# Group 0's head in pieces: a half-and-half load of x and of the modulation weights, q, k and v by half groups, and a new order of all engines

## The chip, the core and the metric

The kernel runs on one core of a Trainium2 chip. The core has five engines with instruction queues of their own: TensorE (PE in the profile; its weight loads are shown as PEld), VectorE (DVE), ScalarE (ACT), GpSimd (POOL) and SyncE (SP), which here issues nearly all DMAs. They run side by side and meet at semaphores. The metric is the device time of one execution in microseconds (us). Three runs of the kernel before gave 236.53, 236.69 and 236.71; their median is 236.69.

## The reference

A transformer block on x of 2048 rows by 512 columns, bfloat16, with six modulation vectors made from a condition vector c:

```
mod = (silu(c) @ w_mod).reshape(1, 6, 1, 512)        # sa, ca, ga, sb, cb, gb
h = layernorm(x) * (1 + ca) + sa
q, k, v = split(h @ wqkv)                            # 32 heads of 16
logits[s, w] = q[s] . k[s - 2 w] / 4,  w = 0..7      # masked where s - 2 w < 0
o = softmax over w, times v[s - 2 w]
x = x + ga * (o @ wo)
h = layernorm(x) * (1 + cb) + sb
x = x + gb * ((gelu(h @ w_gate) * (h @ w_up)) @ w_down)   # 1792 wide
```

The attention looks at eight keys only, at distances 0, 2, ... 14. Its products are made elementwise on VectorE; TensorE sums them over the 16 elements of a head with a 0/1 matrix.

## The kernel before

The 2048 rows are worked in four groups of 512 (`NSG`, `SG`). For each group there is a set of generator functions, each of which yields operations for one engine: statistics and normalisation of the first layernorm (`ln1`, `ln1_x`, `norm_act`), its transposition (`transp0` for group 0, `transp` for the others, by TensorE or by a transposing DMA), scale and shift into `hT` (`transp0_ev`, `transp_ev`), the twelve qkv products of 512 columns (`qkv`, names `qp.group.block.j`), their eviction by ScalarE (`qkv_ev`, names `qkv.group.block.j`), the way of v through DRAM into shifted copies V4 (`vload`), the products of q and shifted k (`logits`, names `pq`), their sums (`logits_mm`, `lp`, tile LTp), softmax (`soft`; `z`, `e`, `s1`, `ri`, `p`), the transposition of the probabilities (`ptp.0` on TensorE for group 0, a store and four loads through DRAM for the others, `est` and `ptl`/`pt`), products with v (`pv`), their sums (`pv_mm`, `o`, tile o_ps), eviction (`oT`), the projection (`x1_mm`, `x1p`), the second layernorm (`LN2`), and the gated MLP: `g` and `u` chunks, gelu on ScalarE (`gl`), a copy (`ub`), their product on VectorE (`hh`), and the down products `y`.

The order of all operations is written out by hand in the list `ORDER`: a sequence of generator numbers. `Issuer.run` takes the next operation of the generator so numbered and emits its instructions, and so each engine's queue has the order in which its operations come up there. The numbers behind `Op(...)` (a duration, a latency) are not used when the kernel is built. `take` and `give` count buffers: `SL["mm"]` is four PSUM banks that qkv, g, u and y share, `SL["att"]` two, `SL["lg"]` one pair.

What matters for the head, group 0, before the change:

- Loads: rows 256 to 511 of group 0 (`x0.2`) are issued on ScalarE's queue, ahead of c; rows 0 to 255 (`x0.0`) on SP's, then the modulation blocks 1 and 0 (ca, then sa; `wm1`, `wm0`, 512 KB each, lines 242 to 245 and 277 to 281), then wqkv0, x1, wqkv1, x2, wqkv2.
- TensorE first multiplies zeros, so that its clock is up (`warmup`, line 217, tile `warm_ps`, twenty matmuls `w0` to `w19`; the last ones are spread between the first useful pieces).
- The modulation products of block 1 and block 0 go into one tile `mp01` (line 348) and are moved with one addition (`mod01`, line 355).
- The rows are normalised and transposed in two halves (`th0`, `th1`, line 509), scaled and shifted in eight evictions of 256 columns, three on ScalarE (line 545) and five on VectorE (line 543).
- Of the qkv products, two of q (j = 0 and 1) are made in halves of 256 columns, sixteen matmuls (`qkv_halves`, line 580); the other ten are made of 512 columns after both halves of `hT` (line 598).

In the order of TensorE, w11 to w15 stand ahead of the first modulation product, then come th0, the second product, w16, th1, w17 to w19 and then the sixteen half matmuls.

Of the kernel before, what the change touches and what calls it, by code (L numbers as in the profile page):

```python
# [106 lines left out]
def kernel(  # L107
# [113 lines left out]
    def loads():  # L221
# [51 lines left out]
        def act_q():  # L273
            yield Op("ACT", 0.46, ldx(0, 2, 4, nc.scalar), fire="x0.2", lat=mb(0.25), dma=True)
            yield Op("ACT", 0.45, ldc, fire="c", lat=0.0, dma=True)
        qs = [act_q()]
        def head_q():
            yield Op("SP", 0.47, ldx(0, 0, 2), fire="x0.0", lat=mb(0.25))
            for b in (1, 0):
                yield Op("SP", 0.5, lambda b=b: ldwm01(b), take=[SL["prod"]] if b else [], fire=f"wm{b}", lat=mb(0.5))  # L280
        qs.append(head_q())
# [12 lines left out]
        def wd_q():  # L294
            for b in range(4):
                yield Op("SP", 0.65, ldwd(b), fire=f"Wd{b}", lat=mb(0.5 if b < 3 else 0.25), after=[f"qp.{g}.{blk}.3" for g in range(NSG) for blk in range(3)])
# [29 lines left out]
    def mods():  # L326
# [15 lines left out]
        for b in (1, 0):  # L342
            def f(b=b):
                if b:
                    B["mp01"] = T("mm", [P, 8], F32, "modT_ps")
                for ch in range(4):
                    for kt in range(4):
                        nc.tensor.matmul(B["mp01"][:, 4 * b + ch:4 * b + ch + 1],  # L348
                                         lhsT=B["wm01"][:, b, kt, ch * P:(ch + 1) * P], rhs=scT[:, kt:kt + 1],
                                         start=(kt == 0), stop=(kt == 3))  # L350
            yield Op("PE", 0.43, f, after=[f"wm{b}", "scT", "w15"], take=[SL["mm"]] if b else [],
                     give=[] if b else [SL["prod"]], fire=f"mp{b}")
# [220 lines left out]
    def qkv_halves():  # L573
# [11 lines left out]
        for j in range(2):  # L585
            pl.done[f"qp.0.0.{j}"] = pl.done["qph.1.3"]
# [391 lines left out]
```

## Time and profile before

| what | us |
|---|---|
| median of three runs | 236.69 (236.53 to 236.71) |
| span of the profiled execution | 234.1 |
| PE busy | 230.0 (98%), 1387 matmuls |
| DVE busy | 170.4 (73%), 240 instructions |
| ACT busy | 150.0 (64%), 283 instructions |
| POOL busy | 18.6 (8%), 43 instructions |
| twenty warm-up matmuls, line 217 | 7.3 busy |
| sixteen half matmuls, line 580 | 2.0 busy |
| qkv matmuls of 512 columns, line 598 | 42.1 busy, 184 of them |

The page gives the span of the profiled execution and no other time of it; what lies around the span is the difference to the runs, about 2.6 us. Times inside a profile count from the start of the span. A line of the chain in order of time has its start, its length and what it was. A line of a timeline has start, length, engine, source line, instruction, the tiles written and read with their shapes, and in brackets how long the engine had been idle before it and what ended that wait. Ends of matmuls are modelled: they are pipelined, so the distance of their starts says more than their length.

### The profile page before, as it was taken

Reading aid. Unit: us, or ns where it says so; the run is one execution under the profiler, and the core shown is the slowest. Engines: PE = TensorE matmul, PEld = TensorE weight load, DVE = VectorE, ACT = ScalarE, POOL = GpSimd, SP = SyncE. Lnnn points to the kernel's source line nnn. Section 1 sums busy time; section 2 is a strip of 40 time slices with the busy share of each in tenths; the row PEclk is TensorE's granted clock in tenths of the full one; section 3 lists DMA queues with packets and bytes.
Section 4 is the critical chain, followed back from the end, with each engine's and each line's share of the span. In section 5 each row is a group of like instructions: output and inputs, shape, how many; then the busy total and the mean of one; then the engine's idle time right before and its main releaser. Section 6 shows DMA issues by size and latency. Waiting matters only on the chain.

```text
span 234.1 us, 3675 instructions
## 1 busy us (share of the span) xinstructions
PE 230.0 (98%) x1387; PEld 108.2 (46%) x1387; DVE 170.4 (73%) x240; ACT 150.0 (64%) x283; POOL 18.6 (8%) x43
## 2 busy tenths in 40 slices
PE   7999999999999999999999999999999999999995
PEld 2755455434644444444444444444444444444443
DVE  3999999999997999999799788467747421222222
ACT  4899997976997758936656492546754343666400
POOL 2612461000100000100000010000001000000000
PEclk9999999999999999999999999999999999999999
DMA  6997989999969839553102963510000411000011
GB/s 218 373 364 213 202 213 171 276 391 303 176 152 236 291 92 200 98 114 103 56 0 57 202 109 60 156 56 0 0 4 0 90 45 45 3 0 0 0 48 45
DMA packets 36265, 30.21 MB, mean 129 GB/s; under 512 B 14872, under 2 KB 34328, under 8 KB 36248
## 3 DMA queue, kind: packets, MB, share of 16 engines
q1 hardware_dynamic: 35968, 29.72, 50.6%
q10 hardware_dynamic: 280, 0.26, 0.3%
q8 instruction: 11, 0.18, 0.3%
q14 instruction: 6, 0.05, 0.1%
HBM read 22.37 MB, written 4.98 MB: 117 GB/s over the span
## 4 chain that ended last, share of the span: by engine, by line
PE 98%; DVE 0%; issue 0%
PE g_ps L844 21%; PE u_ps L844 21%; PE y_ps L856 19%; PE qkv_ps L598 17%; PE x_ps L811 6%; PE o_ps L790 3%; PE LTp L678 3%; PE warm_ps L217 3%; PE y_ps L868 1%; PE qkv_ps L580 1%; PE hTp L484 1%; PE hTp L509 0%; PE modT_ps L305 0%; PE modT_ps L348 0%; PE gR_ps L369 0%; PE PTp L736 0%
## 5 line engine op out<-in xcount | busy, mean ns | idle before, releaser
L844 PE MATMUL g_ps<-h,Wg 128*128 128x512 bf16 x224 | 57.5, 379 | 0.0
L844 PE MATMUL u_ps<-h,Wu 128*128 128x512 bf16 x224 | 57.5, 379 | 0.0
L878 ACT ACTIVATE gl<-g_ps 128x512 bf16<-128x512 f32 x56 | 33.6, 600 | 24.8 <-PE g_ps L844 23.9
L856 PE MATMUL y_ps<-Wd,hht 128*128 128x512 bf16 x210 | 46.0, 379 | 0.0
L885 ACT CAST ub<-u_ps 128x512 bf16<-128x512 f32 x56 | 32.8, 586 | 18.3 <-PE u_ps L844 18.1
L598 PE MATMUL qkv_ps<-hT,wqkv 128*128 128x512 bf16 x184 | 42.1, 380 | 0.0
L896 DVE TENSOR_TENSOR hht<-gl,ub 128x512 bf16<-128x512 bf16 x56 | 23.0, 421 | 25.3 <-ACT ub L885 25.0
L664 DVE TENSOR_TENSOR pq<-qT,kT 128x4096 bf16<-128x4096 bf16 x16 | 36.3, 2292 | 0.0
L771 DVE TENSOR_TENSOR pv<-PT,V 128x4096 bf16<-128x4096 bf16 x16 | 36.0, 2286 | 0.0
L844 PEld LDWEIGHTS <-Wg 128*128 128x128 bf16 x224 | 21.5, 98 | 27.3 <-issue 2.1
L844 PEld LDWEIGHTS <-Wu 128*128 128x128 bf16 x224 | 21.8, 98 | 26.6 <-issue 0.4
L856 PEld LDWEIGHTS <-hht 128*128 128x128 bf16 x210 | 20.5, 98 | 24.8
L598 PEld LDWEIGHTS <-wqkv 128*128 128x128 bf16 x184 | 20.1, 114 | 19.7 <-issue 3.0
L903 DVE TENSOR_TENSOR ot<-y_ps,x 128x512 bf16<-128x512 f32 x15 | 10.3, 689 | 20.2 <-PE y_ps L856 17.2
L471 POOL TENSOR_TENSOR rstd<-rstd,neghalf 128x4 f32<-128x4 f32 (+1 forms) x9 | 8.8, 980 | 154.1 <-DVE rstd L460 85.5
L527 ACT ACTIVATE h<-h,modT,scl 128x512 bf16<-128x512 bf16 x12 | 8.8, 802 | 11.6 <-DMA h<-xn 11.6
L811 PE MATMUL x_ps<-woP,oT 128*128 128x512 bf16 x64 | 15.3, 379 | 0.0
L430 DVE BATCH_NORM_STATS2 st<-x 128x6 f32<-128x512 bf16 x19 | 12.9, 680 | 3.1 <-DMA x<-in_A_x_dram 2.9
L820 DVE TENSOR_TENSOR x<-x_ps,x 128x512 bf16<-128x512 f32 x16 | 10.8, 686 | 5.0 <-PE x_ps L811 5.0
L801 ACT CAST oT<-o_ps 128x512 bf16<-128x512 f32 x16 | 8.9, 592 | 2.7 <-PE o_ps L790 2.7
L618 ACT CAST qT<-qkv_ps 128x512 bf16<-128x512 f32 x16 | 9.2, 587 | 2.2 <-PE qkv_ps L598 2.1
L620 ACT CAST kT<-qkv_ps 128x512 bf16<-128x512 f32 x16 | 9.5, 596 | 1.2 <-PE qkv_ps L598 1.2
(85 smaller groups left out, 181.5 us busy)
## 6 DMA issues: line engine op xcount, KB each, us to landing
V<-vscr SPq DMA_DIRECT2D x12, 520.0 KB, 10.4
wm<-in_w_mod_dram SPq DMA_DIRECT2D x6, 512.0 KB, 5.4
vscr<-vT SPq DMA_DIRECT2D x4, 512.0 KB, 4.2
out_dram<-ot SPq DMA_DIRECT2D x15, 128.0 KB, 1.7
Wg<-in_B_w_gate_dram SPq DMA_DIRECT2D x1, 1792.0 KB, 11.0
Wu<-in_B_w_up_dram SPq DMA_DIRECT2D x1, 1792.0 KB
wqkv<-in_A_wqkv_dram SPq DMA_DIRECT2D x3, 512.0 KB, 8.3
x<-in_A_x_dram SPq DMA_DIRECT2D x3, 512.0 KB, 8.6
```

The lines of the kernel that those rows point to most:

```text
L430: nc.vector.bn_stats(out=st[:], in_=src()[:, c4, :])
L598: nc.tensor.matmul(ps[:], lhsT=wqkv[blk][:, dt, j::4], rhs=B["hT", sg][:, :, dt, :], start=(dt == 0), stop=(dt == DT - 1))
L664: nc.vector.tensor_tensor(out=pq[:], in0=_ap(B["qT", sg][:, j, :], [[0, W], [1, SG]]), in1=_ap(kT[:, j, sg % 3 * SG + 2:sg % 3 * SG + 2 + ...
L771: nc.vector.tensor_tensor(out=t[:], in0=_ap(B["PT", sg][:, 0, :], [[SG, 2], [0, 4], [1, SG]]), in1=_ap(v[:, 0, j, :], [[8, 2], [4 * (SG + ...
L811: nc.tensor.matmul(ps[:], lhsT=B["oT", sg][:, j, c4::CPS] if sg else B["oT", sg][:, j, c4 * P:(c4 + 1) * P], rhs=woP[:, j, :], start=(j == ...
L820: nc.vector.tensor_tensor(out=x[:, c4, :], in0=B["x1ps", sg, c4][:], in1=x[:, c4, :], op=ALU.add)
L844: nc.tensor.matmul(ps[:], lhsT=Wt[:, dt, ft * P:(ft + 1) * P], rhs=B["h2T", sg][:, :, dt, :], start=(dt == 0), stop=(dt == DT - 1))
L856: nc.tensor.matmul(ps[:], lhsT=B["hh", sg, ft][:, c4 * P:(c4 + 1) * P], rhs=B["Wd", ft // 4][:, ft % 4, :], start=(ft == 0), stop=(ft == F ...
L878: nc.scalar.activation(out=gl[:], in_=B["g", sg, ft][:], func=ACT.Gelu_apprx_tanh)
L885: nc.scalar.copy(out=ub[:], in_=B["u", sg, ft][:])
L896: nc.vector.tensor_tensor(out=hh[:], in0=B["gl", sg, ft][:], in1=B["ub", sg, ft][:], op=ALU.mult)
L903: nc.vector.tensor_tensor(out=ot[:], in0=B["y", sg, c4][:], in1=B["x", sg][:, c4, :], op=ALU.add)
```

## The change

- Both halves of group 0's x are issued on SP, rows 0 to 255 first; ScalarE's queue issues only c.
- Blocks 0 and 1 of the modulation weights are loaded together, in two pieces by rows of w_mod (the inner dimension): `wma` holds rows 0 to 255, `wmb` rows 256 to 511, 1024 columns each. Each piece is multiplied into its own PSUM tile (`mpa`, `mpb`), and the two are added one after the other on VectorE (`mod01a`, then `mod01`).
- The second half's transposes of group 0 use `att` banks like the first half's, no longer `mm` banks.
- All twelve qkv products of group 0 are made in halves of 256 columns, `qu.half.block.u`, where u is a pair of j, each pair in one bank, evicted by one copy of 512 elements (`que.half.block.u`). The first of them, `qh.0` to `qh.3`, go through the four dt of half 0 one by one.
- Fifteen warm-up matmuls instead of twenty.
- `ORDER` is another list: the order of all engines and of SP's queue is new. Of the head TensorE now has: w0 to w5, scp (the transposed silu of c), w6 to w13, mpa, mpb, th0, qh.0, qh.1, th1, qh.2, qh.3, qu.0.0.0, qu.0.0.1, w14, qu.1.0.0, qu.0.1.0, qu.1.0.1, qu.1.1.0, qu.0.2.0, qu.0.2.1, qu.1.2.0, qu.1.2.1, the transposes of group 1, qu.1.1.1, qu.0.1.1, lp.0.0. VectorE has x0, va2 (the variance of ScalarE's part), x1, mod01a, x2, mod01, x3 and then the five writes of hT; behind them three statistics of group 1, three of group 2, the x rows of group 1 and only then pq.0.0. SP has x3 ahead of wm2 and wm3, and the store and reload of ga (`gst2`, `ga`) no longer beside group 0's V4 but between group 3's transposing DMA and Wg. Later, LN2.0's transposes stand after all but two qkv chunks of group 3 (before: all but three), and pv.1.0 to pv.1.2 stand ahead of hh.0.4 on VectorE.

```
-        def ldwm01(b):
-            if "wm01" not in B:
-                B["wm01"] = T("prod", [P, 2, 4, D], BF16, "wm01")
-            nc.sync.dma_start(out=B["wm01"][:, b, :, :], in_=w_mod[:, b * D:(b + 1) * D].rearrange("(t p) n -> p t n", p=P))
+        def ldwm01(a):
+            if a == 0:
+                B["wm01"] = T("prod", [P, 4, 2 * D], BF16, "wm01")
+            nc.sync.dma_start(out=B["wm01"][:, 2 * a:2 * a + 2, :],
+                              in_=w_mod[2 * a * P:(2 * a + 2) * P, 0:2 * D].rearrange("(t p) n -> p t n", p=P))
...
+        qs = [one("ACT", 0.45, ldc, fire="c", lat=0.0, dma=True)]
+        qs.append(one("SP", 0.47, ldx(0, 0, 2), fire="x0.0", lat=mb(0.25)))
+        qs.append(one("SP", 0.47, ldx(0, 2, 4), fire="x0.2", lat=mb(0.25)))
...
+        for a in range(2):
+            def f(a=a):
+                B["mp01", a] = T("mm", [P, 8], F32, "modT_ps")
+                for ch in range(8):
+                    for kt in (2 * a, 2 * a + 1):
+                        nc.tensor.matmul(B["mp01", a][:, ch:ch + 1], lhsT=B["wm01"][:, kt, ch * P:(ch + 1) * P],
+                                         rhs=scT[:, kt:kt + 1], start=(kt == 2 * a), stop=(kt == 2 * a + 1))
...
+                nc.vector.tensor_tensor(out=mod01[:], in0=B["mp01", a][:], in1=mod01[:] if a else c01[:], op=ALU.add)
...
-                        ps = T("mm", [P, len(dts), 256], BF16, "hTp") if half else T("att", [P, 2, SG], BF16, "hTp")
+                        ps = T("att", [P, 4, 256], BF16, "hTp")
...
+    def qkv0(half, blk):
+        ev = [f"LN1.0.h{dt}.{half}" for dt in HB[half]]
+        def mm(u, jj, dt, first, last):
+            nc.tensor.matmul(B["qu", half, blk, u][:, jj, :], lhsT=wqkv[blk][:, dt, 2 * u + jj::4],
+                             rhs=B["hT", 0][:, 2 * half:2 * half + 2, dt, :], start=first, stop=last)
...
+        if half == 0 and blk == 0:
+            for n, dt in enumerate(HB[0]):
+                def f(n=n, dt=dt):
+                    for u in range(2):
+                        if n == 0:
+                            B["qu", half, blk, u] = T("mm", [P, 2, 256], F32, "qkv_ps")
+                        mm(u, 0, dt, n == 0, n == DT - 1)
...
+        for u in range(2):
+            def f(u=u):
...
+                for jj in range(1 if half == 0 and blk == 0 else 0, 2):
+                    for n, dt in enumerate(HB[half]):
+                        mm(u, jj, dt, n == 0, n == DT - 1)
...
+    def qkv0_ev(half, blk):
...
+                nc.scalar.copy(out=o, in_=ps[:])
...
-    pl.spawn(warmup(13, 20))
+    pl.spawn(warmup(13, 15))
```

More of the change, by code (lines that the diff above doesn't have):

```diff
@@ L340, in mods, with f @@
                  act="exp", fire="pre")
[L342 to L352, printed above, removed]
-        def f():
-            nc.vector.tensor_tensor(out=mod01[:], in0=B["mp01"][:], in1=c01[:], op=ALU.add)
-        yield Op("DVE", 0.1, f, after=["mp0", "ident"], give=[SL["mm"]], fire="mod01")
+        for a in range(2):
+            def f(a=a):
[4 more added lines that the diff above has]
+                                         rhs=scT[:, kt:kt + 1], start=(kt == 2 * a), stop=(kt == 2 * a + 1))
+            yield Op("PE", 0.43, f, after=[f"wm{'ab'[a]}", "scT"], take=[SL["mm"]], give=[SL["prod"]] if a else [],
+                     fire=f"mp{'ab'[a]}")
+            def f(a=a):
+                nc.vector.tensor_tensor(out=mod01[:], in0=B["mp01", a][:], in1=mod01[:] if a else c01[:], op=ALU.add)
+            yield Op("DVE", 0.1, f, after=[f"mp{'ab'[a]}", "ident"], give=[SL["mm"]], fire="mod01" if a else "mod01a")
     def mods_g(k):
@@ L546, in transp0_ev @@
                 yield Op("DVE" if onv else "ACT", 0.32 if onv else 0.455, f, after=[f"{ev}.th{half}"] + dep,
-                         take=[SL["hT"]] if dt == 0 and half == 0 else [], give=[SL["mm" if half else "att"]] if n == len(dts) - 1 else [],
+                         take=[SL["hT"]] if dt == 0 and half == 0 else [], give=[SL["att"]] if n == len(dts) - 1 else [],
                          fire=f"{ev}.h{dt}.{half}")
@@ L570 @@
     QKV = [(0, 0), (1, 0), (2, 0), (2, 1), (2, 2), (2, 3), (0, 1), (1, 1), (0, 2), (1, 2), (0, 3), (1, 3)]
-    QKV0 = [(0, 0), (0, 1), (0, 2), (1, 0), (1, 1), (0, 3), (1, 2), (2, 0), (2, 1), (2, 2), (2, 3), (1, 3)]
-    def qkv_halves():
-        for half in range(2):
-            for n, dt in enumerate(((2, 0, 3, 1), (0, 1, 2, 3))[half]):
-                def f(half=half, n=n, dt=dt):
-                    for j in range(2):
-                        if half == 0 and n == 0:
-                            B["qkvps", 0, 0, j] = T("mm", [P, SG], F32, "qkv_ps")
-                        nc.tensor.matmul(B["qkvps", 0, 0, j][:, half * 256:half * 256 + 256],
-                                         lhsT=wqkv[0][:, dt, j::4], rhs=B["hT", 0][:, 2 * half:2 * half + 2, dt, :],
-                                         start=(n == 0), stop=(n == DT - 1))
-                yield Op("PE", 0.218, f, after=[f"LN1.0.h{dt}.{half}", "wqkv0"],
-                         take=[SL["mm"]] * 2 + [SL["q"]] if half == 0 and n == 0 else [], fire=f"qph.{half}.{dt}")
-        for j in range(2):
-            pl.done[f"qp.0.0.{j}"] = pl.done["qph.1.3"]
@@ new lines, in qkv0_done, with f @@
+    def qkv0_done():
+        yield Op("PE", 0.0, lambda: None, after=[f"qu.{half}.{blk}.1" for half in range(2) for blk in range(3)], give=[SL["hT"]], fire="qu")
+    def qkv0_ev(half, blk):
+        for u in range(2):
+            def f(u=u):
+                ps = B["qu", half, blk, u]
+                c0 = half * 256
+                if blk == 1:
+                    o = kT[:, 2 * u:2 * u + 2, 16 + c0:16 + c0 + 256]
+                else:
+                    nm = ("qT", "kT", "vT")[blk]
+                    if (nm, 0) not in B:
+                        B[nm, 0] = T(("q", "", "vs")[blk], [P, 4, SG], BF16, nm)
+                    o = B[nm, 0][:, 2 * u:2 * u + 2, c0:c0 + 256]
+                nc.scalar.copy(out=o, in_=ps[:])
+            yield Op("ACT", 0.485, f, after=[f"qu.{half}.{blk}.{u}"], give=[SL["mm"]], fire=f"que.{half}.{blk}.{u}")
@@ L594, in f, with kq @@
+    def kq(sg, blk, j):
+        return [f"qkv.{sg}.{blk}.{j}"] if sg else [f"que.{half}.{blk}.{j // 2}" for half in range(2)]
+    def qkv(sg):
+        for n, (blk, j) in enumerate(QKV):
             def f(blk=blk, j=j):
@@ L601, in qkv @@
             tk = {0: [SL["q"]], 1: [], 2: [SL["vs"]]}[blk] if j == 0 else []
-            yield Op("PE", 0.856, f, after=[f"LN1.{sg}.h{d}" for d in (("0.1", "1.0", "3.1") if sg == 0 else (2, 3))] + [f"wqkv{blk}"], take=[SL["mm"]] + tk,
+            yield Op("PE", 0.856, f, after=[f"LN1.{sg}.h{d}" for d in (2, 3)] + [f"wqkv{blk}"], take=[SL["mm"]] + tk,
                      give=[SL["hT"]] if last else [], fire=f"qp.{sg}.{blk}.{j}")
@@ L626, in qkv_ev @@
                      fire=f"qkv.{sg}.{blk}.{j}")
-        pl.done[f"qkv.{sg}.l"] = pl.done[f"qkv.{sg}.1.3"]
     def halo():
@@ L635, in f @@
             nc.sync.dma_start(out=vscr[:, :, VH + sg * SG:VH + (sg + 1) * SG], in_=B["vT", sg][:])
-        yield Op("SP", 0.65, f, after=[f"qkv.{sg}.2.3"], give=[SL["vs"]], fire=f"vst.{sg}", lat=1.1)
+        yield Op("SP", 0.65, f, after=kq(sg, 2, 3) + kq(sg, 2, 1), give=[SL["vs"]], fire=f"vst.{sg}", lat=1.1)
         for w4 in range(4):
```

46 lines of the change are left out of this document (25 added, 21 removed), and 70 rows, old and new, of the table ORDER.

## The prediction

> **What bounds it now.** I read the page's summary of the chain that ended last, then that chain in order of time, then timelines of VectorE and ScalarE at the places where the chain could be handed over.
>
> ```profile
> span 234.1 us, 3675 instructions
> PE 98%; DVE 0%; issue 0%
> ```
>
> TensorE is 98% of the chain and waits for nobody: a faster kernel must give TensorE less to do, or let its useful work start sooner. The chain in order of time (start, us, what):
>
> ```profile
> 8.98 0.45 PE hTp L509 x8
> 9.43 0.65 PE warm_ps L217 x3
> 10.07 1.85 PE qkv_ps L580 x16
> 11.93 7.77 PE qkv_ps L598 x36
> ...
> 40.04 0.55 PE PTp L736 x16
> 40.59 0.43 PE LTp L678 x8
> ...
> 62.16 0.89 PE hTp L484 x16
> ...
> 80.66 0.97 PE g_ps L844 x4
> 81.63 0.86 PE u_ps L844 x4
> ```
>
> Two things are to be seen. Until 10.07 useful pieces are mixed with `warm_ps` filler. And the work on 32 columns (LTp, o_ps, PTp) costs more at each change of kind: eight matmuls take 0.55 when they follow full-width work and 0.43 when they follow their own kind, and the four matmuls behind them 0.97 where four otherwise take 0.86. A separate run of such work thus costs 0.12 + 0.11 = 0.23 us.
>
> TensorE is not alone. In the stretch from the first statistics of group 1 to the first transposes of LN2, and in the next:
>
> ```profile
> 10.58:62.16 51.58, 51.58 (x380) 26.03 (x378) 50.95 (x66) 44.99 (x100) 10.34 (x8) 1.00 1.02 265
> 62.16:84.50 22.34, 22.34 (x149) 10.42 (x145) 20.84 (x17) 17.68 (x32) 0.00 (x0) 1.00 0.73 196
> ```
>
> (length; busy PE, PEld, DVE, ACT, POOL; clock 1.00; DMA share; GB/s). VectorE is busy 50.95 of 51.58 us. Whatever starts VectorE late here arrives late at every place where TensorE needs it.
>
> **The change, part by part.** (a) *First qkv matmul.* Now:
>
> ```profile
> 4.12 0.69 DVE L430 BATCH_NORM_STATS2 st<-x 128x6 f32<-128x512 bf16 x1 [2.94 <-DMA x<-in_A_x_dram]
> 8.78 0.17 DVE L355 TENSOR_TENSOR mod<-modT_ps,c 128x8 f32<-128x8 f32 x1
> 8.98 1.68 DVE L543 TENSOR_SCALAR hT<-hTp,mod 128x256 bf16<-128x256 bf16 x5
> 10.58 0.69 DVE L430 BATCH_NORM_STATS2 st<-x 128x6 f32<-128x512 bf16 x1
> 9.91 2.02 PE L580 MATMUL qkv_ps<-hT,wqkv 128*128 128x256 bf16 x16
> 2.36 0.51 SPq L223 DMA_DIRECT2D wqkv<-in_A_wqkv_dram  x1
> wqkv<-in_A_wqkv_dram SPq DMA_DIRECT2D x1, 512.0 KB, 6.6
> ```
>
> The two 256 KB halves of x shared the engines until 4.12. With the first half alone in front I put its landing at 3.65 (between 3.4 and no gain, 4.12). VectorE then has the same chain to the first hT write, which took 8.98 - 4.12 = 4.86, plus one more 0.17 add (mod01 is now summed in two steps); the first x row moved ahead of the variance fix-up delays the second rstd by about 0.3, but the last mod matmuls no longer stand behind transposes. I take the first hT write at 8.65, done 0.40 later, so the first qkv matmul at 9.1 instead of 9.91: **-0.81**. It cannot be before wqkv0 lands, 2.36 + 6.6 = 8.96 (-0.95); with no earlier x it is 9.55 (-0.36). The x half that moves from ACT's queue to SP's puts wm and wqkv0 one issue (0.51) later on SP; that is hidden, since wqkv0 lay 6.6 us in a full queue.
>
> (b) *Second-half transposes* now stand behind the first qkv matmuls instead of ahead: +0.45 after that point. (c) One filler, w14, stays there: 0.65/3 = +0.22; the other fillers go, ahead of that point or with it. (d) *256-column matmuls*: 96 instead of 16 of 256 and 40 of 512 columns.
>
> ```profile
> 10.13 1.80 PE L580 MATMUL qkv_ps<-hT,wqkv 128*128 128x256 bf16 x15
> 11.76 7.93 PE L598 MATMUL qkv_ps<-hT,wqkv 128*128 128x512 bf16 x36
> ```
>
> From 10.13 to 11.76 is 15 spacings of 0.109; one of 512 columns is 7.77/36 = 0.216. Each pair of halves costs 0.002 more, 40 pairs +0.06 (bounds: 0; and 0.6 by 1.85/16, which contains the hand-over from a filler). The twelve evictions keep their form and size, so ScalarE's sum stays.
>
> (e) *New order.* I listed the runs of 32-column work in both orders: 15 before, 12 after, all three saved ahead of LN2 (mp2 joins ptp.0; o.0.0 to o.0.3 sit in two runs): 3 x 0.23 = **-0.69** (0 if the saved hand-overs reappear elsewhere).
>
> With TensorE alone: -0.81 + 0.45 + 0.22 + 0.06 - 0.69 = **-0.77**.
>
> (f) *What is given back.* The second half's hT writes on VectorE begin only after its transposes, themselves behind two pairs of qkv matmuls: 9.1 + 0.44 + 0.45 + 0.2 = 10.2, three of them at 1.68/5 = 0.34, so group 1's statistics start at 11.2 against 10.58, 0.6 late. The new order fills one wait (the x rows of group 1 go ahead of the first pq), and 51.58 - 50.95 = 0.63 of slack is there; I let 0.3 of the 0.6 survive (bounds 0 and 0.6).
>
> ```profile
> 38.29 1.22 DVE L722 TENSOR_TENSOR e<-LTp,rinv 128x1024 bf16<-128x1024 f32 x1
> 61.35 0.73 DVE L448 TENSOR_SCALAR xn<-x,mv,rstd 128x512 bf16<-128x512 bf16 x2
> 62.71 2.78 ACT L527 ACTIVATE h<-hTp,modT,scl 128x512 bf16<-128x512 bf16 x4
> 65.83 0.62 ACT L618 CAST qT<-qkv_ps 128x512 bf16<-128x512 f32 x1
> 66.31 0.63 ACT L620 CAST kT<-qkv_ps 128x512 bf16<-128x512 f32 x1
> 66.95 1.28 ACT L878 ACT_TABLE_LOAD   x1
> 68.25 0.60 ACT L878 ACTIVATE gl<-g_ps 128x512 bf16<-128x512 f32 x1
> ```
>
> First place, ptp.0: e ends at 38.29 + 1.22 + 0.3 = 39.81; TensorE, with one of three runs saved, is there at 40.04 - (0.77 - 0.46) = 39.73: **+0.15** with the semaphore. Second, LN2.0: one qkv chunk more (0.86) now stands ahead of its transposes, so TensorE is there at 62.16 + 0.86 - 0.62 = 62.40; VectorE's xn end at 62.08 + 0.3 = 62.38, no wait. But then only two chunks instead of three cover ScalarE, whose chain runs from the transposes to the first gelu: 68.85 - 62.16 = 6.69, less one eviction (66.31 - 65.83 = 0.48), plus 0.1 for a mod4 copy now in front: 6.3. TensorE needs 0.89 + 6 x 0.86 = 6.05 for the work up to the third gate chunk, which needs the bank that gelu frees: **+0.25**. Later rendezvous (o.1.3, o.2.3) I count at nothing, covered by the VectorE idle shown below; without that cover each is worth 0.2 to 0.35.
>
> The other moves: SP issues x3 before wm2 and wm3 (wm2's product moves from behind group 1's transposes to just ahead of ptp.0, so covered); POOL makes its masks after the two rstd (first use is lp.0.0, behind group 0's 7.77 us of qkv from 11.93 on); the tail of the last group keeps its order. Sum: -0.77 + 0.40 = **-0.37**. The trace's execution gives only its span, 234.1; the runs' median, 236.69, stands 2.6 above it, which I leave as it is: **236.3**.
>
> **Rivals.** *VectorE eats it.* If the whole 0.6 survives, ptp.0 waits 0.45, LN2.0 another 0.15 with 0.25 behind it, and one later o group 0.2: -0.77 + 1.05 = +0.3, 237.0. For it: the 50.95 of 51.58. Against: the reordered x rows.
>
> *Nothing is given back.* qkv at 8.96 and no waits: -0.92, 235.8. For it: TensorE waits nowhere in the present order.
>
> *Slower: group 1's attention weights land late.* The store and reload of ga now sit on SP between group 3's transposing DMA and Wg, and SP waits for the store:
>
> ```profile
> SPq L323 <- DMA gscr<-gR: 3.8, 1, 3.8
> 42.30 1.13 SPq L223 DMA_DIRECT2D Wg<-in_B_w_gate_dram  x1
> 67.67 2.53 SPq L758 DMA_DIRECT2D PT<-escr  x4
> PT<-escr SPq DMA_DIRECT2D x4, 64.0 KB, 3.4
> 74.99 0.43 DVE L896 TENSOR_TENSOR hht<-gl,ub 128x512 bf16<-128x512 bf16 x1 [1.30 <-ACT ub L885]
> 75.33 4.49 DVE L771 TENSOR_TENSOR pv<-PT,V 128x4096 bf16<-128x4096 bf16 x2
> ```
>
> (idle of SP's queue; its issues; the loads' median to landing; VectorE.) Everything up to PT runs through this queue, and a wait of up to 3.8 delays Wg by as much. PT's last load is issued by 67.67 + 2.53 = 70.2 and lands 3.4 later, 73.6 at most; the first pv of group 1 now stands ahead of hh.0.4, in the idle 1.30, that is at 74.99 - 1.30 = 73.7 instead of 75.3. So nothing is spare there, and any lateness of PT delays two pv of 4.49, which end at 78.2. TensorE comes to o.1.1 at about 62.16 + 0.89 + 17 x 0.86 - 0.37 + 0.55 + 2 x 0.43 = 78.7, with 0.5 to spare. If half of the 3.8 reaches PT: 1.9 - 0.5 = 1.4 of wait, -0.37 + 1.4 = +1.0, 237.7; it decides from 0.9 of lateness on. Against: the queue has 67.67 - 42.30 = 25 us to catch up.
>
> *Slower: the clock drops.* Gone fillers leave TensorE idle for about 0.5 before the last mod matmuls and 1.0 before the first qkv.
>
> ```profile
> 1.25 4.88 PE L217 MATMUL warm_ps<-gB 128*128 128x512 bf16 x11 [1.25 <-DVE gB L212]
> 6.17 1.25 PE L217 MATMUL warm_ps<-gB 128*128 128x512 bf16 x5
> ```
>
> The first eleven take 4.88/11 = 0.44 each, later ones 0.216: half speed until about 6.1. A second such stretch of 4.9 us costs 2.4: 238.7. The Trainium skill, "TensorE: Matmul & The Clock Gate", Part 1, says the clock is halved again only after an idle window of about 3.4 us; by that rule the idle here is too short and the time stays as summed. The same page's section on a second failure mode says frequent micro-idles between groups can do it as well; by that the 238.7 would come. No run here shows either yet.
>
> **Numbers.** Chances: forecast (-0.1 to -0.75) 0.46; nothing given back (below -0.75) 0.16; VectorE eats it (-0.1 to +0.5) 0.17; PT late 0.15; clock 0.06. About 0.2%, 0.47 us, is what a measurement of this kernel can tell from no change. Half of the forecast's chance and all of the second lie beyond it: faster 0.23 + 0.16 = 0.39; same 0.23 + 0.15 = 0.38; slower 0.23, with a last 0.02 of the VectorE case. The range goes from a little below the no-wait case, 235.7, to 237.3, which leaves out the clock, half of the PT case and a thin lower edge. The likeliest case's own range is 235.9 to 236.6.
>
> **What would show it.** The first 256-column matmul at 9.1 (wrong if later than 9.6); 12 runs of 32-column work; group 1's statistics on VectorE at 11.2; a TensorE wait of 0.1 to 0.3 ahead of PTp and of about 0.25 in the first gate chunks; the granted clock at 1.00 between 6 and 13 us; pv of group 1 starting before 74 without a DMA as its releaser. The prediction is wrong if TensorE shows waits of over 0.8 in sum behind 12 us, or if group 0's qkv waits for wqkv1 or wqkv2, for which I left nothing.

## The result, and the profile after

The changed kernel is slower: 239.82 us (median) against 236.83 for the kernel before on the same chip, a ratio of 1.011 with a 95% interval of 1.0091 to 1.0128. The ratio leaves out the three slowest of the twenty executions (240.57 to 241.16), which are in the median. Forecast were 236.3 and a range up to 237.3. The profiled execution took 240.34, its span 238.6. The page's summary of the chain of the changed kernel:

```profile
span 238.6 us, 3726 instructions
PE 92%; DMA 3%; ACT 2%; SPq 1%; issue 1%; DVE 0%; ACTq 0%
```

TensorE's share fell from 98% to 92%, and waits for loads came in. TensorE's head in the changed kernel (start, length, what, and in brackets the idle time before and what ended it):

```profile
8.02 0.55 PE L347 MATMUL modT_ps<-scT,wm 128*128 128x1 bf16 x16 [1.04 <-DMA wm<-in_w_mod_dram]
9.39 0.57 PE L347 MATMUL modT_ps<-scT,wm 128*128 128x1 bf16 x16 [0.82 <-DMA wm<-in_w_mod_dram]
9.82 1.01 PE L507 MATMUL hTp<-ident,xn 128*128 128x128 bf16 x8
11.33 1.01 PE L577 MATMUL qkv_ps<-hT,wqkv 128*128 128x256 bf16 x4 [0.50 <-DVE hT L541]
```

Two things are to be seen. Both sets of modulation matmuls wait for their load, and the first 256-column matmul starts at 11.33, not at 9.91 as before or at 9.1 as forecast. And the eight transposes take 1.01 where they took 0.70 and 0.61: the clock is down. The stretches between the changes of the granted clock (the share of full speed at which TensorE was let run; then a stretch's length; busy PE and matmuls; clock; DMA share; GB/s):

```profile
6.18:9.60 3.42, 1.56 (x28) 1.00 1.03 378
9.60:13.01 3.41, 2.91 (x35) 0.50 1.06 378
13.01:16.42 3.41, 3.19 (x17) 0.50 1.09 325
16.42:19.84 3.42, 3.42 (x33) 1.00 1.07 255
```

The clock holds for one stretch of 3.41 us in which TensorE was busy for 1.56, and is then 0.50 for two. VectorE and ScalarE at the places where before they were at 10.58, 38.29 and 62.71:

```profile
14.20 0.69 DVE L428 BATCH_NORM_STATS2 st<-x 128x6 f32<-128x512 bf16 x1
42.56 1.21 DVE L750 TENSOR_TENSOR e<-LTp,rinv 128x1024 bf16<-128x1024 f32 x1
67.38 2.79 ACT L525 ACTIVATE h<-hTp,modT,scl 128x512 bf16<-128x512 bf16 x4
```

They are 3.6 to 4.7 us late, and the span ends 4.5 later: 3.6 is there at 14 us, the half clock until 16.42 adds to it, and what lies behind carries it on. (The times differ by less than the spans. The trace of before is one of that kernel's quicker executions, and the trace of after lies 0.5 above its median. What lies around the span is 1.73 to 1.86 us in every execution of the changed kernel and its variants and 2.15 to 2.33 in the others; but here the span ends 1.3 behind the last landing of a DMA and there 1.0, so this is mostly a matter of where the span ends.) So nearly all of the loss arises before 17 us, and the question is why the loads are late. x itself came as forecast, its first half at 3.52. By the trace's landing events (each of a load's 16 DMA engines reports its end, and the last one counts) the modulation's blocks were there at 5.91 and 7.42 in the kernel before; now its halves are at 7.97 and 9.34. The core's DMA engines from 3.5 to 5.5 us, all engines' busy times first, DMA share and GB/s last; the kernel before:

```profile
3.50:5.50 2.00, 2.00 (x7) 0.61 (x5) 1.34 (x3) 0.90 (x3) 0.00 (x0) 1.00 1.08 364
```

The changed kernel:

```profile
3.50:5.50 2.00, 2.00 (x7) 0.68 (x6) 1.85 (x6) 1.26 (x5) 0.00 (x0) 1.00 0.77 205
```

Right behind x the engines moved 205 GB/s instead of 364. And in the kernel before a load's last engine ends about 0.45 us after its first, in the changed kernel 2.3 us after it (wma: first 5.68, last 7.97).

### The profile page after: what moved, and what is told of

Read it like the earlier page. It is cut to its first block, busy times and chain, and to the rows that moved or that the text cites. A ratio compares the mean times of both kernels' runs of the same rounds, so it can differ in the third digit from the quotient of the medians.

```text
span 238.6 us, 3726 instructions
## 1 busy us (share of the span) xinstructions
PE 230.9 (97%) x1409; PEld 113.6 (48%) x1422; DVE 170.2 (71%) x241; ACT 150.2 (63%) x283; POOL 21.8 (9%) x43
## 4 chain that ended last, share of the span: by engine, by line
PE 92%; DMA 3%; ACT 2%; SPq 1%; issue 1%; DVE 0%; ACTq 0%
PE u_ps L872 20%; PE g_ps L872 20%; PE y_ps L884 19%; PE qkv_ps L627 12%; PE x_ps L839 6%; PE qkv_ps L577 5%; PE LTp L706 3%; PE o_ps L818 3%; DMA wm<-in_w_mod_dram 3%; PE y_ps L896 1%; ACT h L525 1%; PE hTp L507 1%; ACT kT L649 0%; ACT LTp L734 0%; SPq L231 0%
## 5 line engine op out<-in xcount | busy, mean ns | idle before, releaser
L924 DVE TENSOR_TENSOR hht<-gl,ub 128x512 bf16<-128x512 bf16 x56 | 22.4, 421 | 25.9 <-ACT ub L913 25.9
L627 PE MATMUL qkv_ps<-hT,wqkv 128*128 128x512 bf16 x144 | 32.3, 380 | 0.0
L469 POOL TENSOR_TENSOR rstd<-rstd,neghalf 128x4 f32<-128x4 f32 (+1 forms) x9 | 11.7, 1304 | 151.1 <-DVE rstd L458 81.2
L627 PEld LDWEIGHTS <-wqkv 128*128 128x128 bf16 x144 | 15.9, 114 | 15.0 <-issue 1.1
L577 PE MATMUL qkv_ps<-hT,wqkv 128*128 128x256 bf16 x96 | 13.1, 299 | 0.7 <-DVE hT L541 0.5
L577 PEld LDWEIGHTS <-wqkv 128*128 128x128 bf16 x96 | 11.0, 119 | 1.9 <-issue 0.6
```

Source lines behind the costliest of these rows:

```text
L469: nc.gpsimd.tensor_tensor(out=k["rstd"][:, a:b], in0=k["rstd"][:, a:b], in1=neghalf[:, a:b], op=ALU.pow)
L577: nc.tensor.matmul(B["qu", half, blk, u][:, jj, :], lhsT=wqkv[blk][:, dt, 2 * u + jj::4], rhs=B["hT", 0][:, 2 * half:2 * half + 2, dt, :], ...
L627: nc.tensor.matmul(ps[:], lhsT=wqkv[blk][:, dt, j::4], rhs=B["hT", sg][:, :, dt, :], start=(dt == 0), stop=(dt == DT - 1))
L924: nc.vector.tensor_tensor(out=hh[:], in0=B["gl", sg, ft][:], in1=B["ub", sg, ft][:], op=ALU.mult)
```

## The experiments

Medians in us; each ratio, with its 95% interval, is to the kernel before, measured beside it (236.67 to 236.83). The orders of TensorE are given by name; "f" is a filler matmul.

**The clock, or the form of the modulation's pieces?** The first theories: the halved clock costs the time (A); the modulation's halves in rows of 2 KB land late and everything follows from that (B); the order behind the head is worse by itself (C). Fillers that keep TensorE busy in the head:

```
-    w13, mpa, mpb, th0, qh.0
+    w13, 4 f, mpa, 4 f, mpb, th0, 2 f, qh.0
```

> The changed kernel with ten more idle-filling matmuls in the head of TensorE's order: four ahead of the first modulation matmuls, four between the two sets, two between the first transposes and the first 256-column matmul. The loads stay as they are. Theory A (the clock: two windows of 3.41 us at half speed because TensorE was busy for only 1.54 of the 3.40 us before them): the granted clock stays at 1.00 from 6 us on, the eight transposes fall from 0.89 to about 0.45, the work from 10.9 to 16.4 runs at full speed and ends about 2.8 us earlier, group 1's statistics start at 11.3 to 11.8 where they started at 14.20; time 236.8 to 237.4, about the kernel before. Theory B (only the late modulation matters, the clock's share is a by-product that something else gives back): 239.0 to 240.0. Theory C (the order behind the head costs it): group 1's statistics early, but 238.5 or more all the same.

Measured: 238.51 (1.0079, 1.0048 to 1.0109). The clock was 1.00 throughout, and 1.3 us came back, about half of what theory A promised. The time is also the one that theory C names (238.5 or more); but C has group 1's statistics early, and they came at 13.31, not at 11.3 to 11.8, so C stays open here. The loads stayed late (modulation at 8.3 and 9.7), and wqkv's last third with them, which TensorE now met:

```profile
PE qkv_ps L577 <- DMA wqkv<-in_A_wqkv_dram: 1.1, 1, 1.1
```

The modulation by blocks of 1 KB rows again:

```
-                in_=w_mod[2 * a * P:(2 * a + 2) * P, 0:2 * D]
+                in_=w_mod[:, b * D:(b + 1) * D]
```

> The changed kernel with the modulation loaded as in the kernel before, one block of 1 KB rows after the other (block 1, then block 0), the matmuls and additions cut to match; no filler is added. Theory B (the halves by rows in 2 KB pieces land late, at about 8.0 and 9.35): the pieces land at about 6 and 7.5, the first 256-column matmul starts at 9.0 to 9.3 where it started at 11.33. If the clock then holds, the time falls by 2 us for the start and 2.8 for the clock, to 235.0 to 236.5. If the order leaves too little work on TensorE even so (theory A alone), the clock still falls at about 9.6 and the time is 237.5 to 238.5. If the place in the queue and not the form of the pieces makes them late, they land at 8.0 and 9.35 again and the time stays at 239.8.

Measured: 239.60 (1.0111, 1.0080 to 1.0142), landings at 8.32 and 9.72. Theory B falls: the halves by rows are as late as the blocks. Blocks and three fillers ahead of qh.0:

> Block loads as in the second kernel and three fillers between the first transposes and the first 256-column matmul. Theories A and B together: the clock is 1.00 from 6 us on, the first 256-column matmul starts by 9.3, group 1's statistics at about 11.2, and the time is 235.0 to 236.5, below the kernel before by what the prediction's ledger gives (about 0.4, up to 1). Theory C (the new order costs by itself): 237 or more with the clock at 1.00.

Measured: 239.89 (1.0129, 1.0091 to 1.0166), landings at 8.6 and 10.1, clock 0.986. The fillers stood behind the late loads and could not help. The kernel before without its last nine fillers:

```
-        pl.spawn(warmup(13, 20))
+        pl.spawn(warmup(13, 11))
```

> The kernel before without its last nine fillers (those behind the silu transposes and around the modulation's matmuls); loads and everything else as they were. TensorE's real work then fills about 2.1 of the 3.41 us from 6.13 on. Theory A: the granted clock falls to 0.5 at about 9.5 for one or two windows and the time grows by 1.5 to 3 us, to 238.3 to 240; if 2.1 us of work are enough to hold the clock, it stays at 1.00 and the time within 0.3 of 236.8, and the bound lies between 1.5 and 2.1. Theory B: no change, 236.8.

Measured: 237.42 (1.0023, 1.0010 to 1.0036): one window at half clock in the profile and a mean clock of 0.991 to 0.993 in all ten executions, but 0.6 us and not 1.5 to 3. The removed fillers had stood in TensorE's way themselves: the first 256-column matmul started at 9.62, earlier than the 9.91 of the kernel before, and only behind it the half clock cost time (the first one of 512 columns at 12.54 instead of 11.76). The window before the drop in this run:

```profile
5.20:8.61 3.41, 2.14 (x42) 1.00 1.04 356
```

**The queue.** Theory D: the head's loads are late because x and the modulation now go through SP's one queue. What e2 still had different from the kernel before in its loads was the queue of rows 256 to 511, and c going first. Only that load put back on ScalarE's queue, behind c:

```
-        qs.append(one("SP", 0.47, ldx(0, 2, 4), ...
+        qs.append(one("ACT", 0.46, ldx(0, 2, 4, nc.scalar), ...
```

> The changed kernel with one load put back: rows 256 to 511 of x go out on ScalarE's queue again (behind c), not on SP's. Theory D (what is late is not due to the form of the modulation's pieces but to the head's loads now all going through SP's one queue: the modulation's transfers end 2.3 to 2.8 us after their first DMA engine has ended, against 0.45 before): the modulation's halves land at about 6 and 7.5, wqkv's first third at about 9, the first 256-column matmul starts at 9.0 to 9.5, and the time is 235.0 to 237.0 if the clock holds, 237.5 to 238.5 if it still halves at about 9.5. Theory B in what is left of it (halves in 2 KB rows are slow by themselves): they land at 8 or later, and the time stays at 239 to 240.

Measured: 238.35 (1.0078, 1.0053 to 1.0103); landings at 5.86, 7.76 and 9.26 (wqkv's first third), as theory D has it. The time is not as D has it: in the profiled execution the clock held, and it took 238.06 where 235.0 to 237.0 were expected; the first 256-column matmul started at 10.64. The same with blocks:

> The same load put back on ScalarE's queue, and the modulation loaded by blocks of 1 KB rows: all loads of the head then have the form, order and queues of the kernel before, but for c going ahead. Theory D: as the run with rows 256 to 511 alone put back, within 0.5 us. If both the queue and the pieces matter: faster than that run by 1 to 2 us. If neither does (the spread of the landings comes from c ahead of the rest, or from the chip): the modulation lands at 8 or later again and 239 to 240.

Measured: 238.59 (1.0083, 1.0055 to 1.0111); 6.00, 7.44, 8.94: no difference. And e5 with three fillers ahead of qh.0:

> Rows 256 to 511 back on ScalarE's queue, and three filler matmuls between the first transposes and the first 256-column matmul. Theories A and D together: clock 1.00 from 6 us on, first 256-column matmul by 9.5, wqkv's last third landed by 15 us so that TensorE does not wait for it, 235.0 to 236.5: the sum of the prediction. Should the order behind the head cost time of its own (theory C), 237 or more with the clock at 1.00 and the loads on time.

Measured: 237.88 (1.0063, 1.0038 to 1.0088). In its profile the clock held and the modulation was on time (5.74 and 7.44), and it still took 237.63. TensorE started its first 256-column matmul at 10.20, because rows 256 to 511, now behind c and beside the modulation, landed at 6.1 (before: 4.4). The other way round, in the kernel before:

```
-            yield Op("ACT", 0.46, ldx(0, 2, 4, nc.scalar), ...
+            yield Op("SP", 0.47, ldx(0, 2, 4), ...
```

> The kernel before with the one load moved the other way: rows 256 to 511 of x from ScalarE's queue to SP's, behind rows 0 to 255, nothing else. Theory D: the modulation's blocks, at 5.9 and 7.4 in the kernel before, land 2 to 2.5 us later with their engines' ends spread over 2 us or more, the first 256-column matmul starts at 11 to 12 where it started at 9.91, and the time grows by 1.5 to 4 us. If the queue does not matter: 236.8 within 0.3, landings as before.

Measured: 238.00 (1.0059, 1.0039 to 1.0078). This one edit moved the modulation from 5.91 and 7.42 to 7.99 and 9.39, the first 256-column matmul from 9.91 to 11.15, and cut the DMA engines' work at the same place as the change did:

```profile
3.50:5.50 2.00, 2.00 (x9) 0.69 (x8) 1.75 (x6) 1.07 (x4) 0.00 (x0) 1.00 0.63 183
```

So the queue of that one load is the cause of the late loads, shown in both directions. All 18 profiles of this case agree: with x and the modulation on SP's queue alone (five) the modulation's first load landed at 7.97 to 8.62, with one of these loads on ScalarE's queue (thirteen) at 5.70 to 6.14. The time grew by 1.2, less than theory D's 1.5 to 4; the clock, behind the fillers that the kernel before has, held in all four executions.

**What the rest is.** The kernel before without the three fillers right ahead of its first 256-column matmul:

> The kernel before without the three fillers (0.65 us) that stand between the second transposes and the first 256-column matmul; no other edit. It tests term (a) by itself: that a start of group 0's q earlier by x gives x. The transposes end at 9.43, h of block 2 is out by about 9.31 and wqkv's first third landed at 8.95, so the first 256-column matmul starts at 9.43 to 9.5 where it started at 9.91, and the time falls by 0.3 to 0.5 us, to 236.3 to 236.5 (ratio about 0.998). The fillers' place is taken by real work, so theory A sees no drop of the clock. If the start is worth nothing (VectorE's chain of group 1 sets the time behind it): 236.8.

Measured: 236.81 (1.0005, 0.9994 to 1.0016). It says little on term (a): in its profile the modulation's second block landed at 7.87 and wqkv's first third at 9.36, so the matmul started at 9.96. Landings between 7.4 and 8.3 occur in profiles whose head loads are the same; the trace that the forecast was summed on had the earliest. The changed kernel with x's rows 256 to 511 first on ScalarE's queue, then c, and three fillers ahead of qh.0:

> The changed kernel with all head loads on the queues of the kernel before (rows 256 to 511 first on ScalarE's queue, then c; rows 0 to 255 and the modulation on SP's), the halves by rows kept, three fillers ahead of the first 256-column matmul, and the silu transpose two fillers later in TensorE's order since c comes later. Against the run with rows 256 to 511 behind c (237.9) it takes away that load's late landing (6.1 there, 4.4 here expected). Theory D with term (a): modulation at about 6 and 7.5, first 256-column matmul at 9.1 to 9.4 (there 10.20), group 1's statistics at 11.2 to 11.5, waits ahead of the logits' products and of PTp below 0.3 in sum; 236.2 to 236.9. If VectorE's order of the new program is what binds from 12 to 42 us (theory C), the waits on VectorE stay at 0.6 or more and the time is 237.2 to 237.9 however early the start.

Measured: 236.97 (1.0004, 0.9994 to 1.0015), although its profile met a late block (8.01) and a window at half clock. The DMA engines are full again:

```profile
3.50:5.50 2.00, 2.00 (x8) 0.57 (x6) 1.46 (x3) 1.06 (x5) 0.00 (x0) 1.00 1.08 370
```

So the queues and the fillers together bring back 2.85 of the 3.0 us. A 32-column run merged, on top of e9 (the second product with Msum beside the third):

> As the run without the three fillers, and with one more edit: the second of group 0's four products with Msum (8 matmuls of 32 columns by themselves at 46.93) moves behind the next four q, k matmuls, beside the third (48.46). One run of 32-column work fewer, priced in the prediction at 0.23 us: 0.2 to 0.25 us below the run without the three fillers, 236.0 to 236.3, a version faster than both kernels. If VectorE waits for the buffer that this product frees 1.5 us later, the gain goes and 236.4 to 236.9 is left.

Measured: 236.74 (1.0000, 0.9991 to 1.0009). The gain went into a new wait on VectorE, as its second case has it:

```profile
PE o_ps L789 <- DVE pv L770: 0.3, 1, 0.3
```

**Where the forecast gain went.** Another load than x's on the second queue (wma on ScalarE's, both halves of x on SP's):

```
-            nc.sync.dma_start(out=B["wm01"][:, 2 * a:2 * a + 2, :],
+            (nc.sync if a else nc.scalar).dma_start(out=B["wm01"][:, 2 * a:2 * a + 2, :],
```

> The changed kernel with another load than x's on the second queue: the first half of the modulation goes out on ScalarE's queue behind c, both halves of x stay on SP's queue, three fillers stand ahead of the first 256-column matmul. If it is one queue for all loads of the head that spreads the landings (theory D in its general form), rows 256 to 511 land at about 4.2, the modulation at about 6 and 7.5 to 8, wqkv's first third by 9.5, the clock stays at 1.00, and the time is 236.3 to 237.2. If only x's load on the second queue helps (something in that transfer, or the place of the modulation behind both halves of x), the modulation lands at 8 or later and the time is 238 to 239.

Measured: 237.29 (1.0023, 1.0013 to 1.0034), modulation at 6.14 and 7.50. So a second queue keeps the modulation on time, whichever of the two loads uses it; but rows 256 to 511 landed at 5.89, later than expected. Terms (b) and (c) taken back, on top of e10:

```
-    th0, 3 f, qh.0, qh.1, th1, ... qu.0.0.1, f, qu.1.0.0
+    th0, 2 f, th1, qh.0, qh.1, ... qu.0.0.1, qu.1.0.0
```

> The run with all head loads on the queues of the kernel before (236.97), with two of the prediction's terms taken back: (b) the second transposes stand ahead of the first 256-column matmul again, in the place of one filler, and (c) the filler among the 256-column matmuls is dropped. By the ledger -0.38 to -0.45 for (b) if the third rows' normalization is out by 8.7, and -0.22 for (c): 236.3 to 236.5, about 0.2% below the kernel before. If VectorE's waits (0.33 and 0.15 ahead of the logits' products and of PTp) grow by what TensorE comes earlier, nothing is gained: 236.9 to 237.1.

Measured: 237.06 (1.0020, 1.0011 to 1.0028): no gain. Not VectorE, as expected for that case, but three others took it: the loads of modulation block 3 (L304) and of the second half (L346), and, in the middle line, the `att` banks of PSUM, which th1 now shares with th0 and gets only when ScalarE has emptied them:

```profile
PE modT_ps L304 <- DMA wm<-in_w_mod_dram: 0.5, 1, 0.5
PE hTp L506 <- ACT hT L542: 0.5, 1, 0.5
PE modT_ps L346 <- DMA wm<-in_w_mod_dram: 0.3, 1, 0.3
```

What holds VectorE in these runs (theory E) is found in its neighbour. GpSimd's reciprocal root of group 2 in e7:

```profile
18.59 3.32 POOL L468 TENSOR_TENSOR rstd<-rstd,neghalf 128x4 f32<-128x4 f32 x1 [2.38 <-DVE rstd L462]
```

and VectorE in the same run:

```profile
18.75 2.29 DVE L691 TENSOR_TENSOR pq<-qT,kT 128x4096 bf16<-128x4096 bf16 x1
21.94 1.06 DVE L445 TENSOR_SCALAR xn<-x,mv,rstd 128x512 bf16<-128x512 bf16 x3 [0.91 <-POOL rstd L468]
```

In the kernel before the same instruction (first for group 1, then for group 2), not beside a pq:

```profile
13.49 1.02 POOL L471 TENSOR_TENSOR rstd<-rstd,neghalf 128x4 f32<-128x4 f32 x1 [3.12 <-DVE rstd L465]
18.30 1.25 POOL L471 TENSOR_TENSOR rstd<-rstd,neghalf 128x4 f32<-128x4 f32 x1 [3.79 <-DVE rstd L465]
```

It lasts until 0.87 after that pq has ended (18.75 + 2.29 = 21.04; 18.59 + 3.32 = 21.91), and VectorE, itself on the chain from 12 to 42 us there, waits 0.91 for it. The eight profiles of versions with a clock at 1.00 or halved for one window, and with this place of the root, all show it (3.31 to 3.32). The changed kernel as given does not, although a pq starts as soon behind the root there:

```profile
21.80 1.11 POOL L469 TENSOR_TENSOR rstd<-rstd,neghalf 128x4 f32<-128x4 f32 x1 [3.34 <-DVE rstd L463]
21.96 2.29 DVE L692 TENSOR_TENSOR pq<-qT,kT 128x4096 bf16<-128x4096 bf16 x1
```

It is the same in e2 and e3, which like it had the clock halved for two windows. What decides between 1.11 and 3.32 is not shown. Two runs on top of e10, one that moves this instruction and drops the late filler, one that only drops the filler:

```
-    VectorE: x.1.0, x.1.1, x.1.2, vd.2, va.2, x.1.3, pq.0.0
+    VectorE: x.1.0, x.1.1, vd.2, va.2, x.1.2, x.1.3, pq.0.0
```

> The run with all head loads on the queues of the kernel before (236.97), with two edits: the late filler among the 256-column matmuls is dropped, and group 2's reciprocal root (the two statistics instructions on VectorE and the 128x4 one on GpSimd) goes two instructions earlier, between the second and third normalized row of group 1, so that it stands less beside VectorE's first pq (2.29 us). Theory E: with its loads on time the changed order is bound from 12 to 42 us by VectorE, and there by that GpSimd instruction, which takes 3.32 us beside pq where it takes 1.02 and 1.25 in the kernel before, leaving VectorE idle for 0.91. Then VectorE's idle time falls to 0.3 to 0.6, its chain and TensorE's waits ahead of the logits' products and PTp shrink by as much, and the time is 0.3 to 0.5 below the run without these edits: 236.4 to 236.7. If that chain does not bind: 236.7 to 237.0, with only the filler or nothing gained.

> The same run with the first of these edits alone: the late filler (0.22) dropped. If TensorE binds, 236.75; by theory E VectorE binds behind it, TensorE only waits 0.2 longer ahead of the logits' products, and the time stays at 236.9 to 237.0.

Measured: 236.38 (0.9985, 0.9969 to 1.0001) and 237.04 (1.0010, 1.0001 to 1.0018). In e14 the instruction took 1.11, VectorE's wait of 0.91 and TensorE's two waits on VectorE were gone:

```profile
19.25 1.11 POOL L468 TENSOR_TENSOR rstd<-rstd,neghalf 128x4 f32<-128x4 f32 x1 [2.06 <-DVE rstd L462]
```

In e15 the 0.22 bought nothing, but its profile names a load for that and not VectorE alone (modulation block 3, lines of TensorE's waits):

```profile
PE modT_ps L304 <- DMA wm<-in_w_mod_dram: 1.0, 1, 1.0
```

In two of e14's twelve executions the clock was still halved for a window (not three, as the next expectation has it); these are its two slowest. Last, e14 with its remaining idle places filled or moved (modulation block 3 goes behind three more products, not four as the expectation has it):

```
-    mpa, mpb, ... lp.0.0, mp3, qp.1.0.0, qp.1.1.0, qp.1.2.0, qp.1.2.1
+    mpa, 3 f, mpb, ... lp.0.0, qp.1.0.0, qp.1.1.0, qp.1.2.0, mp3, qp.1.2.1
```

> The run with group 2's reciprocal root earlier (236.38) with two edits against what its profile still shows: three fillers between the two sets of modulation matmuls, where TensorE idled for 1.21 us (2.20 us of work in that window of 3.41, and the clock halved after it, in three of twelve executions), and modulation block 3's product later, behind four more q and v products of group 1, since its load was 1.0 us late in the run without the late filler. Theories A and E: the clock stays at 1.00, no wait on a modulation load beyond 0.3 us at any place, 235.7 to 236.3, 0.2 to 0.4% below the kernel before. If the clock halves again in some executions even so, the fillers' share of the window is not what decides it, and the median stays at 236.4.

Measured: 235.97 (0.9966, 0.9954 to 0.9978), six executions between 235.81 and 236.17: faster than both kernels. So theory C holds for one place of the order only, the root. The page's chain and TensorE's head in it:

```profile
PE 95%; ACT 2%; issue 0%; DVE 0%; ACTq 0%
```

```profile
7.18 0.81 PE L217 MATMUL warm_ps<-gB 128*128 128x512 bf16 x3
7.97 0.55 PE L347 MATMUL modT_ps<-scT,wm 128*128 128x1 bf16 x16
9.50 0.60 PE L577 MATMUL qkv_ps<-hT,wqkv 128*128 128x256 bf16 x4
```

Here the second half of the modulation landed at 7.93 and wqkv's first third at 9.42, no earlier than in e10, and the view of TensorE's waits holds only the one for its first operand.

## Why the prediction was wrong

- **The step that failed** is the last sentence of (a): the x half on SP's queue "puts wm and wqkv0 one issue (0.51) later on SP; that is hidden". The issue was hidden, the transfers were not. I took a load's duration from its row and thought only of when it is issued; the first 512 KB of the modulation took 6.2 us from issue to landing instead of 4.6 once no second queue fed the DMA engines beside SP's. I had no run of this kernel with a single queue, so the cost was unknown and should have been bounded, not set to nothing. Alone in the kernel before it is +1.2 (e8), with the clock held.
- **The rival "the clock drops"**, which I gave 0.06, came true on top of it. Fillers that held the clock brought back 1.3 of the 3.0 us (e1). I argued that the idle was too short, by pricing 0.5 and 1.0 us of idle against 3.4; with the loads late it was 1.0 and 0.8, and already 1.2 us less work in a window was enough. What the drop alone costs stays open: I took 2.4 for a stretch of 4.9 us, and in e1 the loads were late still. Of the changed kernel's twenty executions the two with a mean clock of 0.998 or more took 236.99 and 237.84, the seven at 0.991 to 0.993 a median of 239.40, the eleven at 0.984 to 0.986 one of 240.34; whether the loads were late in the first two no profile shows.
- **x earlier**: its first half landed at 3.52 (forecast 3.65). That part of (a) was right and of no use here. The start at 9.1 was reached in no run: with the queues of the kernel before and the clock held, e15 and e16 start at 9.52 and 9.50, right behind the landing of wqkv's first third (9.39 and 9.42).
- **(b), (c)**: th1 and the filler show in TensorE's order as priced. Putting th1 back gained nothing: three waits took it, one of them for its new banks (e13), a cost of the change of banks that I had not seen.
- **(d)**: 256-column matmuls follow each other in 0.109 us, as taken.
- **(e)**: three runs of 32-column work fewer ahead of LN2, as listed. From the first 256-column matmul to LN2.0's transposes TensorE needs 52.09 us in the kernel before (9.91 to 62.00) and 52.77 in e16 (9.50 to 62.27), where it waits for nothing and has no late filler. With th1's 0.45, (d)'s 0.06 and the further qkv chunk's 0.86 taken off, 0.69 less is left, as forecast.
- **(f)**: the wait ahead of PTp is there (0.15 in e7 and e10), but the number is luck. Group 1's statistics do start 2.09 behind the first 256-column matmul, as in the forecast (e7 and e16); but from them to e VectorE needs 27.71 us in the kernel before, 28.02 in e10 and 27.02 in e14. So the new order alone would have made good the late start, and the wait comes from a term that was missing: GpSimd's root of group 2 beside a pq, 0.91 us of VectorE. With the root moved the wait is gone (e14, e16). At LN2.0 the forecast 0.25 was near: by the distance of starts four matmuls take 0.86, and in e16 the first gate chunk takes 1.14, since its last matmul starts 0.28 late, about when ScalarE ends h; another 0.07 is lost ahead of the third chunk, where I had put all of it.

```profile
64.89 1.30 PE L872 MATMUL g_ps<-h,Wg 128*128 128x512 bf16 x4
66.03 1.02 PE L872 MATMUL u_ps<-h,Wu 128*128 128x512 bf16 x4
```

- **The rival "PT late"** did not come: in e16 group 1's first pv starts at 73.34 (before: 75.33), and no DMA releases it.
- **The end**: with the head's queue restored, the clock held and the root moved, the same order reaches 235.97, 0.8 below the kernel before (e16). The sum "TensorE alone", -0.77, has that size, but not that make-up. Against the trace of the kernel before, e16's start gained 0.41 of the 0.81 in (a); with (b), (d), (e) and the 0.35 at LN2.0 that makes -0.24, and the third gate chunk starts 0.26 earlier and the last DMA lands 0.28 earlier. Most of the other half of the 0.8 is that the trace the forecast was summed on was a quick execution of the kernel before (span 234.1; the median span beside e16 is 234.55). That its slower ones lose by loads that land late, and e16 does not (start at 9.50 with such a load), is likely but not shown.

What stays open: why one queue alone feeds the engines worse at this place. The runs show that it does, and that either of two loads on the second queue cures it; they do not show the mechanism. Open are also what the halved clock costs by itself, and what decides whether the root is held up.

## What to carry to other kernels

A load that is moved from one queue to another is a change of the transfer and not only of its issue: look at the DMA share right behind it and at the spread of the engines' ends, and try a second queue in a head that waits for its first loads. Count TensorE's work in each window of the clock, not its longest pause, and put fillers where the loads can be late, ahead of the waiting matmuls, not behind them. When a new order gains nothing, look for a small instruction of a neighbouring engine that now stands beside a long one.

## What the runs showed of the hardware

- **The granted clock** changes only at steps of 3.41 us, whose phase to the program differs from run to run (the first full-speed window began between 4.2 and 7.3 us). At full clock, windows with 1.41, 1.47, 1.56, 2.14 (e4), 2.16 and 2.20 us of matmuls were followed by half clock; windows with 1.97 and 2.14 (e5), 2.18, 2.29 and more were not. The two sets overlap, so the busy time alone does not decide. From half clock, windows with 2.08, 2.29 (e3) and 2.91 us did not bring it back, those with 3.19 and more did. So one kernel runs with and without the drop: of twenty executions of the changed kernel, two kept a mean clock of 0.998 or more. e5's two windows, side by side:

```profile
4.91:8.32 3.41, 2.14 (x36) 1.00 1.07 384
8.32:11.74 3.42, 1.97 (x32) 1.00 1.06 383
```

  The Trainium skill, "TensorE: Matmul & The Clock Gate", Part 1, gives the window (3413 ns, running free of the kernel's start), and these traces agree; it has the clock fall after an idle window of about 3.4 us, and here it fell after windows up to 64% full (2.20 of 3.41) with no pause over 2.0 us. The measurement decides.
- **Queues**: the Trainium skill, "DMA: Bandwidth & Descriptors", section "Issuing engines are not separate DMA queues", says that issuing from several engines saves only the time to initiate a DMA. In this head it was worth 1.2 us (e8): 183 instead of 364 GB/s from 3.5 to 5.5 us once one 256 KB load had left the second queue. The measurement decides.
- **GpSimd beside VectorE**: 3.32 us instead of 1.0 to 1.25 for a 128x4 instruction beside a 128x4096 bfloat16 product of 2.29, in eight profiles; 1.11 in three others, though the product starts 0.16 behind it there too. A later root beside a pq takes 3.03 to 3.08 in every profile of the changed order (1.01 in the kernel before), and nothing waits for it. In all these slow cases the end lies 0.86 to 0.87 behind the product's. The Trainium skill, "SBUF — State Buffer", section "Terms", has the two share a port pair that is locked for a whole instruction; 3.32 - 2.29 = 1.03, the time that the instruction takes alone, agrees with that, and the three profiles with 1.11 are not explained by it.
